# Weight rounding in a top-k attention and MLP kernel: the power of two by an exponential in bfloat16 on ScalarE

## The chip, the cores and the metric

The kernel runs on one core of a Trainium2 chip. The metric is the device time of one execution in microseconds, as the median of several runs. TensorE (PE) multiplies matrices, VectorE (DVE) and ScalarE (ACT) work element by element, GpSimd (POOL) does the same more slowly, and SyncE (SP) issues the DMA transfers.

## The reference, cut to what matters

```
scores = q @ k.T / sqrt(64)              # 8 batches x 8 heads, 576 x 576
keep the 32 largest of each row, softmax over them
attn_out = attn @ v                      # laid out as x: 4608 tokens x 512
h = x @ w_in                             # 512 x 2048
out = maximum(0.01 * h, h) @ w_out       # 2048 x 512
```

The inputs `w_in` and `w_out` arrive as 64-bit floats; the others are used as 32-bit floats. The kernel rounds the two weight matrices to 32 bits on the chip. This rounding is where the change lies.

## The kernel before, in words

**Three stages.** First the weights are loaded and rounded. Then 144 units of attention (128 query rows of two heads each) go through scores, top 32, softmax, transposition and the product with `v`. Whenever the tokens of a chunk (128 or 256) are complete, the MLP runs on them. The order of instructions on every engine is written out by hand: each engine works through its own queue in the order in which the program emits instructions, and waits on semaphores where data or buffers are missing. The MLP's matmuls are spread between those of attention by a budget, so that TensorE is fed throughout.

**Weight rounding.** `round_weights(n)` handles one of 16 pieces of 128 x 1024 values (pieces 0 to 7 are `w_in`, 8 to 15 `w_out`). Each 64-bit value arrives as four 16-bit words, 1 MB for a piece, in one of three `raw` buffers. The value is put together again as mantissa times a signed power of two:

- L119, GpSimd: the topmost word (sign, 11 bits of exponent, 4 bits of mantissa) is copied to `top`. It has two buffers, so the copy of piece n waits until piece n - 2 is done with it (L146).
- L120 and L122, ScalarE: the middle and the two low words become floats, in `dst` and `m_low`.
- L124, VectorE: shift and mask give the exponent, a number from 0 to 2047, as a 16-bit integer in `scale`.
- L126, VectorE: it is clamped to 896 to 1151, the range for which a power of two can be made by shifting bits.
- L128, ScalarE, pieces 0 to 13: (exponent - 896) x 128 is the bit pattern of that power of two in bfloat16. For pieces 14 and 15 VectorE does this (L130).
- L131 and L132, VectorE: the top mantissa bits as a bfloat16 between 1 and 2, and the sign bit alone.
- L142 to L144, TensorE: three matmuls with scaled identities add up the three parts of the mantissa in PSUM.
- L146 and L149, VectorE: sign and power of two are joined by an or, and the mantissa sum from PSUM is multiplied by the result.

**The order around it.** The loop at L484 interleaves three pieces. In step n the program emits piece n's part up to the first `yield` (L119 to L122), piece n - 1's part up to the second (L124 to L144), and piece n - 2's rest (L146, L149); then SP's queue gets the load of piece n + 3. So on VectorE one step is L124, L126, L131, L132 of one piece, then L146 and L149 of the piece before. On ScalarE it is L120 and L122 of one piece, then L128 of the piece before. The load of piece n + 3 takes the `raw` buffer of piece n, and waits until L119, L120 and L122 of piece n have read it.

In steps 6 to 9 the loads of four pairs of q and k (L162, L163, 0.59 MB a pair) stand in SP's queue behind the weights'. In step 13 `first_scores` of the first unit is emitted (TensorE L230, ScalarE copies L235), and in step 16 that of the second. The first `top_k` (VectorE, L244 to L252) stands behind the last L149 in VectorE's queue.

Of the kernel before, what the change touches and what calls it, by code (L numbers as in the profile page):

```python
# [1 line left out]

# [6 lines left out]
F32 = mybir.dt.float32  # L9
U32 = mybir.dt.uint32  # L10
U16 = mybir.dt.uint16
BF16 = mybir.dt.bfloat16
AF = mybir.ActivationFunctionType
ALU = mybir.AluOpType
# [5 lines left out]
def kernel(  # L20
# [13 lines left out]
    nc = tc.nc  # L34
    NPAIR, P, S = qT.shape
# [22 lines left out]
    const = ctx.enter_context(tc.tile_pool(name="const", bufs=1))  # L58
# [13 lines left out]
    ident_low = const.tile([P, P], BF16, name="ident_low")  # L72
    nc.vector.tensor_scalar(ident_low, ident, 2.0 ** -23, None, ALU.mult)

    w_in = [const.tile([P, DFF], F32, name=f"w_in{c}") for c in range(HP)]
    w_out = [const.tile([P, 4, DMODEL], F32, name=f"w_out{c}") for c in range(NFC // 4)]
    gT = const.tile([P, NFC, CHMAX], F32, name="gT")
# [3 lines left out]
    NPIECE = 2 * HP * DFF // WCH  # L81
# [3 lines left out]
    def piece(n):  # L85

        if n < NPIECE // 2:
            j, c = divmod(n, HP)
            return w_in[c][:, j * WCH:(j + 1) * WCH]
        f = 2 * (n - NPIECE // 2)  # L90
        return w_out[f // 4][:, f % 4:f % 4 + 2, :].rearrange("p g n -> p (g n)")
# [12 lines left out]
    def round_weights(n):  # L104

        raw = raw_of.pop(n)  # L110
        dst = piece(n)
        mid = raw[:, :, 2]
        low = raw.rearrange("p n w -> p (n w)").bitcast(U32).rearrange("p (n w) -> p n w", w=2)[:, :, 0]
        top = raws.tile([P, WCH], U16, name="top", bufs=2)
        scale = raws.tile([P, WCH], U16, name="scale", bufs=2)
        parts = work.tile([P, 2 * NKC - 1, P], F32, name="wT", bufs=3)
        parts = parts.rearrange("p c n -> p (c n)").bitcast(U16)
        m_top, m_low = parts[:, 0:WCH], parts[:, WCH:2 * WCH].bitcast(BF16)
        nc.gpsimd.tensor_copy(top, raw[:, :, 3])  # L119
        nc.scalar.activation(dst, mid, AF.Copy, bias=-7.0 - 2.0 ** -16, scale=2.0 ** -20)  # L120

        nc.scalar.activation(m_low, low, AF.Copy, bias=128.0, scale=2.0 ** -29)  # L122
        yield
        nc.vector.tensor_scalar(scale, top, 4, 0x7FF, ALU.logical_shift_right, ALU.bitwise_and)  # L124

        nc.vector.tensor_scalar(scale, scale, 1151.0, 896.0, ALU.min, ALU.max)  # L126
        if n < NPIECE - 2:
            nc.scalar.activation(scale, scale, AF.Copy, bias=-896.0 * 128, scale=128.0)  # L128
        else:
            nc.vector.tensor_scalar(scale, scale, 896.0, 128.0, ALU.subtract, ALU.mult)  # L130
        nc.vector.tensor_scalar(m_top, top, 0xF, 0x3F80, ALU.bitwise_and, ALU.bitwise_or)  # L131
        nc.vector.tensor_scalar(top, top, 0x8000, None, ALU.bitwise_and)  # L132
        if n < NPIECE - 4 or n % 2 == 0:
            tag, bufs = ("wide", 2) if n < NPIECE - 4 else ("narrow", 1)
            pw = ps_sc.tile([P, 2, 512], F32, name=tag, bufs=bufs)
            sums = [(pw[:, h, :], h * 512) for h in range(2)]
            ends = [(pw.rearrange("p h n -> p (h n)"), 0)]
        else:
            ends = sums = [(ps_ml.tile([P, 512], F32, name="pw", tag="ml"), h * 512) for h in range(2)]
        for pw, c in sums:  # L140
            at = slice(c, c + 512)
            nc.tensor.matmul(pw, ident_top, m_top[:, at].bitcast(BF16), start=True, stop=False)  # L142
            nc.tensor.matmul(pw, ident, dst[:, at], start=False, stop=False)
            nc.tensor.matmul(pw, ident_low, m_low[:, at], start=False, stop=True)  # L144
        yield
        nc.vector.tensor_tensor(scale, scale, top, ALU.bitwise_or)  # L146
        for pw, c in ends:
            at = slice(c, c + pw.shape[-1])
            nc.vector.tensor_tensor(dst[:, at], pw, scale[:, at].bitcast(BF16), ALU.mult)  # L149
# [319 lines left out]
    with tc.manual_schedule():  # L469
# [14 lines left out]
        for n in range(NPIECE + 2):  # L484
            for i in (n, n - 1, n - 2) if AS_WORDS else ():
                if 0 <= i < NPIECE:
                    if i == n:
                        rounding[i] = round_weights(i)
                    next(rounding[i], None)
            load_weights(n + 3)  # L490
            if 6 <= n < 6 + HP:
                load_qk(n - 6)
            elif n == NPIECE - 3:
                first_scores(steps[0])
            elif n == NPIECE:
                first_scores(steps[1])
            if n == NPIECE - 1:
                load_v(0)
                load_v(1)
# [132 lines left out]
```

## Time and profile before

| | before |
|---|---|
| median of 6 runs | 1476.02 us (1474.91 to 1477.42) |
| the profiled execution | 1476.83 us |
| its span in the trace | 1475.0 us |
| mean granted clock of TensorE | 0.981 |
| TensorE busy | 1392.9 us (94%) |
| VectorE busy | 1328.3 us (90%) |
| ScalarE busy | 1096.4 us (74%) |
| GpSimd busy | 1097.1 us (74%) |
| HBM read, written | 46.14 MB, 92.60 MB |
| L126, 16 instructions | 427 ns each, at 7.1 to 63.9 us |
| L128, 14 instructions | 1052 ns each |
| table loads on ScalarE | 1, 1283 ns, at 0.71 us |

How to read it: the span is what the hardware profiler recorded from the first instruction to the last, and the execution's own time is a little longer. Busy time is an average over three very different stages, so a stage has to be looked at by itself: a row of the timeline gives start, duration, engine, line, operation and, in brackets, how long the engine was idle before and what ended that.

### The profile page before, as it was taken

How to read it: one execution, taken by the hardware profiler on the slowest of the kernel's cores; microseconds unless marked ns; L12 is line 12 of the kernel's file. 1: busy time of each engine (PE TensorE's matmuls, PEld its weight loads, DVE VectorE, ACT ScalarE, POOL GpSimd, SP SyncE). 2: the span in 40 equal slices, each digit the busy share in tenths (PEclk: the TensorE clock that was granted, in tenths of full speed). 3: DMA queues.
4: the chain of work that ended last, by engine and by line, in shares of the span. 5: the costliest groups of instructions: out<-in, count | busy, mean ns of one | idle time of the engine just before them, and what ended most of it. 6: DMA issues, size and time to landing. Idle time of an engine off the chain costs nothing.

```text
span 1475.0 us, 24095 instructions
## 1 busy us (share of the span) xinstructions
PE 1392.9 (94%) x8059; PEld 926.5 (63%) x8059; DVE 1328.3 (90%) x3414; ACT 1096.4 (74%) x1979; POOL 1097.1 (74%) x742
## 2 busy tenths in 40 slices
PE   6715989999999999999999999999999999999998
PEld 2303547676766767676767666767676767676674
DVE  7999999999999999999999999999999999999600
ACT  8647887877788787877787877787877787877720
POOL 2278887887788888788878887888788888788700
PEclk9967999999999999999999999999999999999999
DMA  8724453655367464565566545575557556554510
GB/s 324 304 59 132 138 144 93 183 141 156 100 176 207 135 150 133 171 186 148 139 164 193 150 126 145 163 204 138 135 164 208 134 142 132 165 134 137 144 47 14
DMA packets 391420, 223.48 MB, mean 152 GB/s; under 512 B 336256, under 2 KB 336256, under 8 KB 389248
## 3 DMA queue, kind: packets, MB, share of 16 engines
q1 hardware_dynamic: 391296, 221.95, 53.8%
q8 instruction: 63, 1.03, 0.3%
q14 instruction: 61, 0.50, 0.1%
HBM read 46.14 MB, written 92.60 MB: 94 GB/s over the span
## 4 chain that ended last, share of the span: by engine, by line
PE 86%; DVE 12%; DMA 1%; issue 1%; ACT 0%; POOL 0%; DVEq 0%; ACTq 0%
PE pz L390 33%; PE ph L378 32%; PE wide L327 11%; PE wide L214 6%; DVE tops L249 4%; PE narrow L214 3%; DVE pairs L252 3%; DVE pairs L244 1%; DVE w_out L149 1%; DMA wT<-apart 1%; DVE w_in L149 1%; DVE scale L146 1%; DVE scale L124 0%; DVE scale L126 0%; DVE top L132 0%
## 5 line engine op out<-in xcount | busy, mean ns | idle before, releaser
L262 POOL TENSOR_SCALAR pen<-s_sb,tops 128x576 f32<-128x576 f32 x288 | 638.1, 2216 | 208.6 <-DVE tops L249 122.2
L249 DVE MAX8 tops<-pairs 128x8 f32<-128x288 f32 (+1 forms) x1152 | 635.9, 591 | 0.0
L390 PE MATMUL pz<-w_out,gT 128*128 128x512 f32 x1152 | 508.4, 596 | 0.0
L378 PE MATMUL ph<-x,w_in 128*128 128x256 f32 x2176 | 481.1, 381 | 0.0
L252 DVE MATCH_REPLACE8 pairs<-tops,pairs 128x288 f32<-128x288 f32 (+1 forms) x864 | 460.1, 538 | 0.0
L378 PEld LDWEIGHTS ph<-x,w_in 128*128 128x128 f32 x2176 | 410.7, 190 | 77.1 <-issue 22.9
L263 POOL TENSOR_TENSOR s_sb<-s_sb,pen 128x576 f32<-128x576 f32 x288 | 406.6, 1412 | 24.0
L390 PEld LDWEIGHTS pz<-w_out,gT 128*128 128x128 f32 x1152 | 215.3, 190 | 266.2 <-issue 264.3
L287 ACT COPY split<-s_sb 128x1152 uint16<-128x1152 uint16 x282 | 309.1, 1144 | 0.0
L278 ACT ACTIVATE s_sb<-s_sb,rz 128x576 f32<-128x576 f32 x288 | 207.0, 769 | 41.0 <-DVE rz L275 40.9
L266 ACT ACTIVATE s_sb<-s_sb,nbias 128x576 f32<-128x576 f32 x288 | 220.9, 767 | 12.5 <-POOL s_sb L263 12.5
L244 DVE TENSOR_TENSOR pairs<-s_sb 128x576 f32<-128x576 f32 x288 | 213.7, 780 | 9.9
L327 PEld LDWEIGHTS wide<-wT,vt 128*64 128x64 f32 x3200 | 160.8, 139 | 67.3 <-ACT s_sb L221 26.5
L327 PE MATMUL wide<-wT,vt 128*64 128x128 f32 (+1 forms) x3200 | 178.2, 268 | 24.6 <-ACT s_sb L221 21.8
L384 ACT ACTIVATE gT<-ph 128x512 f32<-128x512 f32 x136 | 80.6, 593 | 80.0 <-PE ph L378 80.0
L341 ACT COPY x<-wide 128x128 f32<-128x128 f32 (+1 forms) x160 | 32.1, 260 | 129.5 <-PE wide L327 129.4
L221 ACT COPY s_sb<-wide 128x704 f32<-128x704 f32 x142 | 107.1, 754 | 23.7 <-PE wide L214 23.6
L214 PE MATMUL wide<-kt,qt 64*128 64x352 f32 (+1 forms) x392 | 75.9, 503 | 27.2 <-ACT s_sb L221 23.6
L221 ACT COPY s_sb<-narrow 128x448 f32<-128x448 f32 x142 | 68.7, 536 | 1.3 <-PE narrow L214 0.7
L397 ACT COPY o_sb<-pz 128x512 f32<-128x512 f32 x36 | 21.1, 585 | 59.3 <-PE pz L390 59.3
L275 DVE RECIPROCAL rz<-ze 128x2 f32<-128x2 f32 x144 | 22.4, 155 | 45.4 <-ACT ze L271 45.2
L252 DVE MATCH_VALUE_LOAD pairs<-tops,pairs 128x8 f32 x864 | 62.6, 72 | 0.0
(62 smaller groups left out, 623.8 us busy)
## 6 DMA issues: line engine op xcount, KB each, us to landing
apart<-split SPq DMA_DIRECT2D x282, 288.0 KB, 2.1
raw<-in_weights_dram SPq DMA_DIRECT2D x16, 1024.0 KB, 6.2
vt<-in_vk_dram SPq DMA_DIRECT2D x32, 320.0 KB, 3.3
out_dram<-o_sb SPq DMA_DIRECT2D x36, 256.0 KB, 2.0
qt<-in_qT_dram SPq DMA_DIRECT2D x20, 288.0 KB, 3.3
kt<-in_kT_dram SPq DMA_DIRECT2D x20, 288.0 KB, 3.6
raw<-in_qT_dram SPq DMA_DIRECT2D x12, 288.0 KB, 3.2
raw<-in_kT_dram SPq DMA_DIRECT2D x12, 288.0 KB, 3.5
```

What stands on the lines that cost most here:

```text
L214: nc.tensor.matmul(to[r0:r0 + u.rows, i, :], qt[d, u.q0:u.q0 + u.rows], kt[d, k0:k1], start=True, stop=True)
L244: nc.vector.tensor_tensor(pairs[:, :, n, :], u.both[:, :, 0:HS], u.both[:, :, HS:S], op)
L249: nc.vector.max(out=u.tops[:, i, r, :], in_=rest[i])
L252: nc.vector.match_replace(out=rest[i], in_to_replace=u.tops[:, i, r, :], in_values=rest[i], imm_value=LOWEST)
L262: nc.gpsimd.tensor_scalar(pen, u.s[i], u.tops[:, i, ROUNDS - 1, 7:8], MASKED, ALU.is_lt, ALU.mult)
L263: nc.gpsimd.tensor_tensor(u.s[i], u.s[i], pen, ALU.add)
L266: nc.scalar.activation(u.s[i], u.s[i], AF.Exp, bias=u.nbias[:, i:i + 1], scale=SCALE, accum_out=u.z[:, i:i + 1])
L278: nc.scalar.activation(u.s[i], u.s[i], AF.Copy, bias=0.0, scale=u.rz[:, i:i + 1])
L287: nc.scalar.copy(split, pairs[:, :, h])
L327: nc.tensor.matmul(po[side * D:(side + 1) * D, o, :], vt[:, c, side, :], u.wT[:, c + side * NKC if c + 1 < NKC else c, r:r + n], start=(c ...
L378: nc.tensor.matmul(ph[:, i, 0:n], w_in[c][:, f * P:(f + 1) * P], x[c][:, 0:n], start=(c == 0), stop=(c == HP - 1),)
L390: nc.tensor.matmul(pz[0:m, 0:DMODEL], gT[:, f, r0:r0 + m], w_out[f // 4][:, f % 4, :], start=(f == 0), stop=(f == NFC - 1),)
```

## The change

ScalarE now computes 2 to the power (exponent - 1023) as an exponential, exp(ln 2 x exponent - 1023 ln 2), and writes it into the same 16-bit words as a bfloat16 number; before, it computed the bit pattern as an integer. The bias is read from a new 128 x 1 tile, `least`, that GpSimd fills once at the start. The clamp on VectorE remains only for pieces 14 and 15, whose power of two VectorE makes by bits as before.

```
+    LN2 = math.log(2.0)
+    least = const.tile([P, 1], F32, name="least")
+    nc.gpsimd.memset(least, -1023.0 * LN2)
...
         nc.vector.tensor_scalar(scale, top, 4, 0x7FF, ALU.logical_shift_right, ALU.bitwise_and)
-
-        nc.vector.tensor_scalar(scale, scale, 1151.0, 896.0, ALU.min, ALU.max)
         if n < NPIECE - 2:
-            nc.scalar.activation(scale, scale, AF.Copy, bias=-896.0 * 128, scale=128.0)
+
+            nc.scalar.activation(scale.bitcast(BF16), scale, AF.Exp, bias=least, scale=LN2)
         else:
+
+            nc.vector.tensor_scalar(scale, scale, 1151.0, 896.0, ALU.min, ALU.max)
             nc.vector.tensor_scalar(scale, scale, 896.0, 128.0, ALU.subtract, ALU.mult)
```

More of the change, by code (lines that the diff above doesn't have):

```diff
@@ L1 @@
+import math
 from contextlib import ExitStack
```

## The prediction

> **What bounds the kernel now.** I read the page's busy slices first, then the windows view by stage, the wait view of TensorE, the timeline of the weight stage engine by engine, the weight stage's waits, and last the groups of ScalarE.
>
> First the page's busy tenths in 40 slices of 36.9 us, then two rows of the windows view (busy us and counts of PE, PEld, DVE, ACT, POOL, then granted clock, DMA share, GB/s).
>
> ```profile
> PE   6715989999999999999999999999999999999998
> ...
> DVE  7999999999999999999999999999999999999600
> ```
>
> ```profile
> 70.00:140.00 70.00, 21.71 (x152) 15.45 (x151) 69.48 (x182) 40.78 (x76) 52.98 (x37) 0.66 0.31 85
> ...
> 200.00:1365.00 1165.00, 1159.30 (x7031) 792.89 (x7031) 1119.51 (x2916) 917.10 (x1696) 948.45 (x635) 1.00 0.57 153
> ```
>
> Three stages follow one another. The weights are rounded until 69.4 us. Then VectorE picks the first top 32 without a gap (69.48 of 70 us) while TensorE waits for it (21.71 of 70 us busy). From about 140 us TensorE is the full engine: 1159.30 of 1165 us, and the chain that ended last is its matmuls. Nothing between 70 us and the end is tied to an absolute time: the first `top_k` starts behind the last L149 on VectorE, and TensorE's long stretch starts behind the first `top_k`s. A weight stage that ends x us earlier should end the program x us earlier, so the question is what paces this stage.
>
> The timeline of one step of it (start us, duration, engine, line, idle before), for VectorE, ScalarE and GpSimd:
>
> ```profile
> 33.14 0.43 DVE L124 TENSOR_SCALAR scale<-top 128x1024 uint16<-128x1024 uint16 x1
> 33.60 0.43 DVE L126 TENSOR_SCALAR scale<-scale 128x1024 uint16<-128x1024 uint16 x1
> 33.94 0.42 DVE L131 TENSOR_SCALAR wT<-top 128x1024 uint16<-128x1024 uint16 x1
> 34.40 0.43 DVE L132 TENSOR_SCALAR top<-top 128x1024 uint16<-128x1024 uint16 x1
> 34.74 0.69 DVE L146 TENSOR_TENSOR scale<-scale,top 128x1024 uint16<-128x1024 uint16 x1
> 35.53 1.23 DVE L149 TENSOR_TENSOR w_in<-wide,scale 128x1024 f32<-128x1024 f32 x1
> 36.87 0.43 DVE L124 TENSOR_SCALAR scale<-top 128x1024 uint16<-128x1024 uint16 x1
> ```
>
> ```profile
> 34.06 1.06 ACT L128 ACTIVATE scale<-scale 128x1024 uint16<-128x1024 uint16 x1 [0.57 <-DVE scale L126]
> 35.03 1.14 ACT L120 ACTIVATE w_out<-raw 128x1024 f32<-128x1024 uint16 x1
> 36.08 1.12 ACT L122 ACTIVATE wT<-raw 128x1024 bf16<-128x1024 uint32 x1
> ```
>
> ```profile
> 35.49 1.14 POOL L119 COPY top<-raw 128x1024 uint16<-128x1024 uint16 x1 [2.58 <-DVE scale L146]
> ```
>
> VectorE has no gap: its step is 36.87 - 33.14 = 3.73 us, and L126 holds 33.60 - 33.14 = 0.46 of it (0.43 of work and the wait for its own predecessor's result). ScalarE is idle 0.57 us in it, waiting for L126.
>
> Waits of the weight stage, ScalarE's timeline at its end, and a row of the windows view there:
>
> ```profile
> ACT w_out L120 <- DMA raw<-in_weights_dram: 2.7, 3, 1.2
> ...
> DVE scale L146 <- ACT scale L128: 0.2, 1, 0.2
> ```
>
> ```profile
> 51.51 1.14 ACT L120 ACTIVATE w_out<-raw 128x1024 f32<-128x1024 uint16 x1 [1.17 <-DMA raw<-in_weights_dram]
> ...
> 53.60 1.04 ACT L128 ACTIVATE scale<-scale 128x1024 uint16<-128x1024 uint16 x1
> 56.97 1.18 ACT L235 COPY s_sb<-wide 128x576 f32<-128x576 f32 x2 [2.32 <-PE wide L230]
> ...
> 60.11 1.07 ACT L128 ACTIVATE scale<-scale 128x1024 uint16<-128x1024 uint16 x1
> ```
>
> ```profile
> 40.00:45.00 5.00, 3.66 (x11) 1.17 (x9) 4.58 (x9) 3.74 (x4) 1.51 (x2) 1.00 1.04 416
> ```
>
> The reader is to see two near limits. Pieces 11 to 13 come late to ScalarE (three waits, 2.7 us), because four q/k pairs are loaded between them and the 16 DMA engines are full (share 1.04 at 416 GB/s). And the last ACT L128, of piece 13, ends at 60.11 + 1.07 = 61.18 us, just before the L146 that needs it (VectorE's timeline: 61.26).
>
> **The change, part by part.** The profiled execution took 1476.83 us (span 1475.0, 1.83 around it), 0.81 over the median of 1476.02; gains are worked out in its trace and taken from the median.
>
> *VectorE loses 14 x L126.* L131 does not read `scale`, so it will follow L124 as it now follows L126, after 0.34 us; each piece's step falls by 0.46 to 3.27 us. The ceiling is 14 x 0.46 = 6.4 us. Piece 0's share counts, through TensorE: its matmuls start behind L131 and end when L149 may begin (13.22 us). Piece 1's does not: VectorE then waits for ScalarE (the 0.2 us row) and for those matmuls. From piece 2 each counts, so L124 of piece n comes 0.46 x (n - 1) earlier: piece 12 by 5.06, at 46.69; piece 13 by 5.52, at 49.95.
>
> *ScalarE's copy becomes an exponential with a bias read from a tile* (groups of instructions: count, busy us, mean ns, idle before).
>
> ```profile
> L266 ACT ACTIVATE s_sb<-s_sb,nbias 128x576 f32<-128x576 f32 x288 | 220.9, 767 | 12.5 <-POOL s_sb L263 12.5
> ...
> L306 ACT COPY wT<-wide 128x1024 f32<-128x1024 f32 x3 | 3.0, 1012 | 2.6 <-PE wide L300 2.6
> ...
> L306 ACT COPY wT<-wide 128x128 f32<-128x128 f32 x3 | 0.8, 277 | 0.0
> ```
>
> No exponential of 1024 elements from 16-bit words is in the trace. The nearest row is L266, an exponential with a bias tile, 767 ns for 576; the two L306 rows give (1012 - 277) / 896 = 0.82 ns an element, so 767 + 448 x 0.82 = 1134 ns against L128's 1052: +0.08. Bounds: 1012 ns (L306, -0.04) and 1182 ns (the longest L120, +0.13). When ScalarE doesn't wait, its step is 3.02 us (L128 at 16.17 to L128 at 19.19); it becomes 3.10, still under 3.27. The 0.08 is covered by what is left of ScalarE's idle time, 0.17 a step; without that cover it is 14 x 0.08 = 1.1 us.
>
> *A memset of 128x1 on GpSimd.* L619's memsets take 0.10 us, and GpSimd sits idle from 1.3 to 5.5 us for the first transfer; without that cover, 0.1 us. The exponential also waits for it, 8 us after it is done. The exponential's other wait moves from L126 to L124, so it is shorter; behind it in ScalarE's queue stand the next piece's L120 and L122, and L146 waits for it.
>
> *What comes earlier with it.* TensorE's share of a step is 2.75 us (34.42 to 37.18), under 3.27. GpSimd's copy waits for L146, and L124 for the copy: 1.14 + 0.69 + the VectorE work between is 3.55 of 3.73 now and shrinks by the same 0.46. SP issues the load of piece n + 3 when copy n has ended, with the q/k loads queued behind it. Piece 9's load is issued with copy 6, at 29.2 us, now 5 x 0.46 = 2.3 us earlier (pieces 0 and 2 to 5). From it on the DMA engines are full: the landings of pieces 11, 12 and 13 (43.24, 47.22, 51.51 us, where ScalarE resumed) are 4.1 us apart for a piece and a pair, 1.64 MB, which is 400 GB/s. So these landings come only 2.3 us earlier: piece 12 at 44.92, piece 13 at 49.21, while VectorE would want them 5 us earlier. The slack that hid this shrinks away:
> - Piece 12: L120, L122 and the exponential of piece 11 end 2.09 + 1.13 us after landing (2.09 is 51.51 to 53.60), at 48.14. VectorE would reach L146 at 46.69 + 1.14 = 47.83. Stall 0.35.
> - Piece 13: exponential of piece 12 ends at 49.21 + 3.22 = 52.43. VectorE reaches L146 at 51.55 (L124 at 50.41, behind GpSimd's copy). Stall 0.92; L146 at 52.47 instead of 57.07, gain 4.6.
> - The clamp of piece 13 is gone from VectorE, where L124 of piece 14 follows at 54.60 and L146 could start at 56.67. ScalarE's queue (exponential 12, two copies L235, L120, L122, exponential 13) ends at 51.30 + 1.05 + 1.06 + 1.06 + 1.02 + 1.13 = 56.62. They tie: no further stall.
>
> The weight stage ends 4.6 us earlier, and the median becomes 1476.02 - 4.6 = 1471.4.
>
> One rule of the Trainium skill speaks against that rate. The page "DMA: Bandwidth & Descriptors", section "Where 436 GB/s comes from", puts loads from HBM at about 358 GB/s for a core; here the 40 to 45 us row has 416, so the measurement decides. By the page's figure piece and pair would take an estimated 4.6 us instead of 4.1, pieces 11 to 13 would land 1 to 2 us later and the gain would be near 3.
>
> **The rivals.**
> - *The transfers keep up.* If the loads, asked for earlier, land as much earlier (the share of 0.76 to 0.94 before 35 us is some room), only ScalarE's queue at piece 13 is left: VectorE's gain at L149 of piece 11 is 12 x 0.46 = 5.5, less 0.08: 5.4 us, and up to 6.4 if that queue has slack. 1470.6, at best 1469.6. Against: the share stands at 0.96 to 1.04 from 35 us.
> - *The transfers decide all.* If ScalarE's chain behind piece 13's landing has no slack beyond the 2.3 us that L146 had (landing + 5.56 now, 3.26 needed), or the DMA engines lose rate, the gain is only the landings' own shift, 2.3: 1473.7.
> - *It doesn't arrive at the end.* TensorE has 98% of its work from 140 us on; if its written-out order gives the gain back in new waits (it has 7 us of waits from 200 us on), the time stays at 1476.
> - *Slower: the exponential and the copies evict each other's tables.* Place: ScalarE, between L122 and L128. A table load took 1.28 us at the start; two for each of 14 pieces make ScalarE's step 3.10 + 2.56 = 5.66 us, against VectorE's present 3.73: some 13 x 1.9 = 25 us, 1501. It decides from 0.63 us of extra ScalarE work a piece (3.73 - 3.10). Against: the page has one table load in a program with 288 exponentials between copies and Prelus. The Trainium skill, "ScalarE: Activation LUTs", section "What ACT_TABLE_LOAD costs", prices every switch at 2.66 us, by which two a piece would be an estimated 5.3 us a piece.
>
> **How the numbers follow.** My forecast (gain 3.5 to 5.1) 0.58; transfers keep up 0.18; transfers decide 0.13; nothing arrives 0.06; slower 0.05. About 0.2% (3 us) is what a measurement of this kernel can tell from no change. Faster by more: 0.58 + 0.18 = 0.76. Within: 0.13 + 0.06 = 0.19. Slower: 0.05. The range goes from the ceiling (1469.6) less 0.2 for the runs' spread to the transfers' case (1473.7) and 0.3 more: 1469.4 to 1474.0, which leaves out the last two cases and edges.
>
> **What would show it.** Right: no L126 but two; L124 to L124 3.27 us apart between pieces 3 and 10; the exponential at 1.1 to 1.2 us; one table load; VectorE's L146 waiting for ScalarE once or twice, about 1.3 us in all, near 48 and 52 us; `top_k`'s first L244 at 64.8 instead of 69.42. Wrong: a step that stays above 3.4 us, further table loads, waits of several us for `raw`, or a first L244 that is early with an end that isn't.

## The result and the profile after

| | before | after |
|---|---|---|
| median | 1475.69 us (36 runs) | 1473.04 us (18 runs, 1470.64 to 1473.93) |
| ratio to before | | 0.9978, 95% interval 0.9972 to 0.9984 |
| the profiled execution, its span | 1476.83, 1475.0 us | 1473.77, 1471.8 us |
| first `top_k` instruction on VectorE | 69.42 us | 66.01 us |
| from there to the end of the span | 1405.6 us | 1405.8 us |

The change makes the kernel 0.22% faster, about 3.2 us (2.4 to 4.1 by the interval); the two medians alone are 2.65 us apart. The forecast was a gain of 4.6 us. All of the gain is made before the first `top_k`, where 3.4 of the forecast 4.6 us arrived; the rest of the program lasts as long as before. The diff adds lines: the exponent's shift is now L129, the exponential L132, the mantissa bits L137, the sign L138, the or L152, the product L155, the first `top_k` line L250, and on ScalarE L120 and L122 are L125 and L127.

The busy tenths on the page after:

```profile
PE   7716989999999999999999999999999999999998
...
DVE  6899999999999999999999999999999999999600
```

And the windows view (busy us and counts of PE, PEld, DVE, ACT, POOL; clock, DMA share, GB/s):

```profile
70.00:140.00 70.00, 21.88 (x133) 14.70 (x130) 69.38 (x180) 41.13 (x76) 55.99 (x38) 0.66 0.34 93
200.00:1365.00 1165.00, 1162.37 (x7043) 795.12 (x7042) 1119.11 (x2918) 916.00 (x1694) 949.11 (x635) 1.00 0.57 153
```

The three stages are the same: VectorE without a gap behind the weights, then TensorE full.

VectorE's timeline of one late step of the weight stage, after (start us, duration, engine, line, idle before):

```profile
43.99 0.43 DVE L129 TENSOR_SCALAR scale<-top 128x1024 uint16<-128x1024 uint16 x1
44.33 0.42 DVE L137 TENSOR_SCALAR wT<-top 128x1024 uint16<-128x1024 uint16 x1
44.79 0.43 DVE L138 TENSOR_SCALAR top<-top 128x1024 uint16<-128x1024 uint16 x1
45.77 0.69 DVE L152 TENSOR_TENSOR scale<-scale,top 128x1024 uint16<-128x1024 uint16 x1 [0.55 <-ACT scale L132]
46.56 1.23 DVE L155 TENSOR_TENSOR w_out<-wide,scale 128x1024 f32<-128x1024 f32 x1
47.89 0.43 DVE L129 TENSOR_SCALAR scale<-top 128x1024 uint16<-128x1024 uint16 x1
```

The clamp is gone, and L137 follows L129 after 0.34 us. But this step is 3.90 us long: the or L152 waits for ScalarE's exponential. The waits of the stage, after:

```profile
ACT w_out L125 <- DMA raw<-in_weights_dram: 3.4, 5, 0.8
...
DVE scale L152 <- ACT scale L132: 2.6, 4, 0.8
...
DVE scale L129 <- DVE w_in L155: 0.5, 1, 0.5
```

ScalarE's timeline shows what the exponential waited for: it stands behind L125 and L127 of the next piece, and these wait for its transfer (pieces 10 to 13).

```profile
38.52 1.15 ACT L125 ACTIVATE w_out<-raw 128x1024 f32<-128x1024 uint16 x1 [0.78 <-DMA raw<-in_weights_dram]
...
42.51 1.17 ACT L125 ACTIVATE w_out<-raw 128x1024 f32<-128x1024 uint16 x1 [0.74 <-DMA raw<-in_weights_dram]
...
46.50 1.15 ACT L125 ACTIVATE w_out<-raw 128x1024 f32<-128x1024 uint16 x1 [0.76 <-DMA raw<-in_weights_dram]
...
50.40 1.15 ACT L125 ACTIVATE w_out<-raw 128x1024 f32<-128x1024 uint16 x1 [0.70 <-DMA raw<-in_weights_dram]
```

They are 4.0 us apart, and VectorE's steps behind them 3.9 to 4.0. The loads themselves take longer from issue to landing (least, median and longest of the 16 weight pieces, before and then after):

```profile
DMA to landing us min/median/max: 4.7/6.2/8.9
```

```profile
DMA to landing us min/median/max: 4.9/7.1/9.6
```

### The profile page after: what moved, and what is told of

It reads as the page before. It is cut to its first block, busy times and chain, and to the rows that moved or that the text cites. A ratio compares the mean times of both kernels' runs of the same rounds, so it can differ in the third digit from the quotient of the medians.

```text
span 1471.8 us, 24082 instructions
## 1 busy us (share of the span) xinstructions
PE 1394.1 (95%) x8059; PEld 927.6 (63%) x8059; DVE 1322.4 (90%) x3400; ACT 1097.3 (75%) x1979; POOL 1097.1 (75%) x743
## 4 chain that ended last, share of the span: by engine, by line
PE 84%; DVE 11%; DMA 3%; ACT 1%; issue 1%; SPq 0%; POOL 0%; DVEq 0%; ACTq 0%
PE pz L396 32%; PE ph L384 31%; PE wide L333 10%; PE wide L220 6%; DVE tops L255 4%; PE narrow L220 3%; DVE pairs L258 3%; DMA wT<-apart 1%; DVE pairs L250 1%; DMA raw<-in_weights_dram 1%; ACT split L293 1%; DMA apart<-split 1%; DVE w_in L155 1%; DVE w_out L155 0%; DVE scale L152 0%
## 5 line engine op out<-in xcount | busy, mean ns | idle before, releaser
L250 DVE TENSOR_TENSOR pairs<-s_sb 128x576 f32<-128x576 f32 x288 | 213.4, 779 | 10.0
L347 ACT COPY x<-wide 128x128 f32<-128x128 f32 (+1 forms) x160 | 32.1, 260 | 129.9 <-PE wide L333 129.9
L258 DVE MATCH_VALUE_LOAD pairs<-tops,pairs 128x8 f32 x864 | 62.5, 72 | 0.0
```

What stands on the lines that cost most here:

```text
L250: nc.vector.tensor_tensor(pairs[:, :, n, :], u.both[:, :, 0:HS], u.both[:, :, HS:S], op)
L258: nc.vector.match_replace(out=rest[i], in_to_replace=u.tops[:, i, r, :], in_values=rest[i], imm_value=LOWEST)
```

## The experiments

The theory: VectorE's step did fall by 0.46 us, and the landings of the weight pieces, held up by the four q/k pairs among them, took part of it back (transfers theory). The main rival: the dearer exponential holds up VectorE's or (ScalarE theory). Beside the medians, the table gives the start of the first `top_k` in the profiled execution, which shows the stage alone and is not blurred by the 1405 us behind it. It is the start in one execution, and that need not be a typical one: E3's and E6's profiled executions were the slowest of their runs, E7's and E9's the fastest, 1.2 to 2.7 us from the median. Each ratio is to the kernel before in the same session, whose median was 1475.41 us for E1 to E4, 1475.01 for E5 to E8 and 1474.86 for E9 and E10, so medians of different sessions are not to be compared as they stand.

| kernel | median us | ratio to before, interval | first `top_k` us | from there to the span's end |
|---|---|---|---|---|
| E1 no clamp, integer copy | 1471.96 | 0.9979, 0.9969 to 0.9988 | 65.96 | 1404.1 |
| E2 clamp, exponential | 1475.43 | 1.0001, 0.9992 to 1.0011 | 69.58 | 1404.8 |
| E3 change, late pairs | 1470.77 | 0.9968, 0.9956 to 0.9979 | 65.18 | 1404.9 |
| E4 before, late pairs | 1475.15 | 0.9997, 0.9988 to 1.0006 | 69.64 | 1405.2 |
| E5 change, no sign | 1472.78 | 0.9983, 0.9974 to 0.9992 | 67.11 | 1404.2 |
| E6 no sign, late pairs | 1470.34 | 0.9965, 0.9953 to 0.9977 | 64.19 | 1405.7 |
| E7 change, late pairs, new order | 1468.63 | 0.9956, 0.9944 to 0.9969 | 61.46 | 1404.1 |
| E8 as E7, no clamp at all | 1468.08 | 0.9954, 0.9940 to 0.9967 | 61.85 | 1404.4 |
| E9 change, new order | 1471.34 | 0.9977, 0.9968 to 0.9986 | 63.16 | 1403.7 |
| E10 before, late pairs, new order | 1470.85 | 0.9973, 0.9964 to 0.9982 | 64.66 | 1404.8 |

**E1 and E2: the two halves of the change alone.**

```
E1, on the change:
-            nc.scalar.activation(scale.bitcast(BF16), scale, AF.Exp, bias=least, scale=LN2)
+            nc.scalar.activation(scale, scale, AF.Copy, bias=-896.0 * 128, scale=128.0)
E2, on the change:
+        nc.vector.tensor_scalar(scale, scale, 1151.0, 896.0, ALU.min, ALU.max)
         if n < NPIECE - 2:
...
-            nc.vector.tensor_scalar(scale, scale, 1151.0, 896.0, ALU.min, ALU.max)
```

> The clamp of the first 14 pieces is gone, and ScalarE keeps its integer copy instead of the exponential. Transfers theory (the landings of pieces 9 to 13 cap the gain): the same time as the change, about 1473 (-2.7 to -3.2 against before), since the exponential's 0.08 us sits beside waits for landings; at most 0.3 us better, from three copies that stand behind a landing. ScalarE theory (the exponential's price holds VectorE's L152 up): the full 5.4 us, 1470.3.

> The exponential alone: VectorE keeps all 16 clamps. Transfers theory: VectorE's step stays 3.73 us and ScalarE's 3.10 is hidden in it, so 0 to +0.2 us against before, about 1475.8. ScalarE theory: slower by 14 x 0.08 = 1.1 us or more.

E1's ratio and its first `top_k` are those of the change (0.9979 and 0.9978; 65.96 and 66.01), and E2 is the kernel before (1.0001). Leaving out the clamp is worth everything; making the power of two by an exponential changes the time by nothing that these runs can tell. The ScalarE theory falls. The exponential's group in the profile after:

```profile
L132 ACT ACTIVATE scale<-scale,least 128x1024 bf16<-128x1024 uint16 x14 | 16.0, 1140 | 0.0
...
L125 ACT ACT_TABLE_LOAD x1 | 1.3, 1283 | 0.7 <-PEq L625 0.7
```

It takes 1140 ns, and there is still one table load.

**E3 and E4: three pairs loaded behind the last weight piece.**

```
-            if 6 <= n < 6 + HP:
-                load_qk(n - 6)
-            elif n == NPIECE - 3:
+            if n == 6:
+                load_qk(0)
+            elif NPIECE - 4 <= n < NPIECE - 1:
+                load_qk(n - (NPIECE - 5))
+            if n == NPIECE - 3:
                 first_scores(steps[0])
```

> The change, with the q/k pairs 1 to 3 (1.77 MB) loaded behind the last weight piece instead of between pieces 10 and 13. Transfers theory: the waits for landings of pieces 10 to 13 go, VectorE's step stays 3.26 us to piece 12, the first top_k instruction starts at 64.0 +- 0.4 instead of 66.01, and the time is 1475.7 - 5.4 = 1470.3. If the landings were late for another reason than these pairs (late already at pieces 6 to 9), about half of that: first top_k at 65, 1472. ScalarE theory: no change from 1473.

> The kernel before, with the same three pairs loaded behind the last weight piece. Transfers theory: ScalarE's waits for landings (2.7 us) go, but VectorE paced the stage, so the time stays within 0.4 us of 1475.7. If the transfers had cost the kernel before something too, it is 1 to 2 us faster.

E4 is the kernel before (0.9997): with the clamp, VectorE hid the transfers. E3 gains 4.7 us instead of 3.2, though the intervals of the two ratios overlap. But for 0.42 us at piece 9 its steps stay at 3.26 us to piece 14, whose L129 comes at 53.60 us instead of 55.78 in the change, and ScalarE's waits for pieces from 8 on fall from 3.4 to 1.2 us. So the late landings cost the change about 2.2 us at that point. Not all of this is the pairs' doing: up to piece 9 the two kernels load the same, and yet piece 9 took 5.2 us from issue to landing in E3's execution and 7.4 in the change's (more of this below). But the first `top_k` came at 65.18, not at 64.0. Part of it was lost at the end, where TensorE's timeline in E3 shows the last piece:

```profile
60.10 0.49 PE L148 MATMUL pw<-wT,ident_top 128*128 128x512 bf16 x1 [2.00 <-DVE wT L137]
60.38 1.92 PE L149 MATMUL pw<-w_out,ident 128*128 128x512 f32 x2
62.09 0.63 PE L150 MATMUL pw<-wT,ident_low 128*128 128x512 bf16 x1
```

The windows view of E3 at the same place:

```profile
58.00:60.00 2.00, 0.10 (x1) 0.00 (x0) 1.83 (x5) 0.21 (x1) 0.04 (x1) 1.00 1.03 399
60.00:62.00 2.00, 1.90 (x3) 0.69 (x3) 1.86 (x4) 0.00 (x0) 0.00 (x0) 0.56 1.05 403
62.00:64.00 2.00, 2.00 (x5) 0.92 (x4) 1.73 (x3) 0.00 (x0) 0.00 (x0) 0.59 1.04 393
```

TensorE idled 2.00 us for the last piece's mantissa bits, its granted clock fell to 0.56 to 0.59 (means of 2 us), and two matmuls of L149 took 1.92 us where they take 1.02 otherwise. VectorE waited 0.74 us for them, 0.42 us for the exponential of piece 13, and 0.42 us once more at L129 of piece 9 (told of below). Without these three, 65.18 would be 63.6.

**E5 and E6: one more instruction less on VectorE, with the pairs among the weights and behind them.**

```
-        nc.vector.tensor_scalar(top, top, 0x8000, None, ALU.bitwise_and)
+        if n >= NPIECE - 2:
+            nc.vector.tensor_scalar(top, top, 0x8000, None, ALU.bitwise_and)
...
-        nc.vector.tensor_tensor(scale, scale, top, ALU.bitwise_or)
+        nc.vector.tensor_tensor(scale, scale, top, ALU.bitwise_or if n >= NPIECE - 2 else ALU.bitwise_and)
```

> The change, and for pieces 0 to 13 also without the instruction that isolates the sign bit (the or behind it becomes an and, so the weights' scales are not the reference's). VectorE's step would fall by another 0.46 us, to 2.80. Transfers theory: the landings of pieces 9 to 13 pace the stage already, so the first top_k instruction stays at 65.0 to 66.0 us (66.01 in the change) and the time at 1472.0 to 1473.0. If VectorE still paced most of the stage: first top_k near 61, 1468.

> The same with q/k pairs 1 to 3 behind the last weight piece. VectorE's step 2.80, so ScalarE's 3.12 or the transfers of one piece in 3.2 us pace it. Transfers theory: first top_k 1.0 to 2.5 us earlier than the 65.18 of the run with late pairs and the sign kept. ScalarE theory says the same with 3.12 a piece: 16 pieces end at about 63.5. If neither bounds it: 60.

For pieces 0 to 13 these two kernels leave out the isolation of the sign, so their weights are not the reference's; only their time is of use. E5 has 14 x 0.46 us less to do on VectorE than the change, and its first `top_k` starts no earlier: 67.11 us, later than the forecast 65 to 66 even; the time is that of the change. What VectorE no longer does it waits, as its row in the waits of E5 shows:

```profile
DVE scale L153 <- ACT scale L132: 9.0, 13, 1.3
```

Thus VectorE did not pace the stage any more. In E6 the first `top_k` came at 64.19, 1.0 earlier than E3's, at the lower end of what was expected; VectorE there waits 0.23 us for ScalarE in most steps, whose own step is 3.12 us. So three limits lie close together: VectorE's 3.26, ScalarE's 3.12, and the transfers.

**E7 and E8: VectorE makes the mantissa bits first.** E7 is E3 with one line moved; E8 also drops the last two clamps.

```
E7, on E3:
+        nc.vector.tensor_scalar(m_top, top, 0xF, 0x3F80, ALU.bitwise_and, ALU.bitwise_or)
         nc.vector.tensor_scalar(scale, top, 4, 0x7FF, ALU.logical_shift_right, ALU.bitwise_and)
...
-        nc.vector.tensor_scalar(m_top, top, 0xF, 0x3F80, ALU.bitwise_and, ALU.bitwise_or)
E8, on E7:
-            nc.vector.tensor_scalar(scale, scale, 1151.0, 896.0, ALU.min, ALU.max)
```

> Late pairs, and VectorE makes the mantissa bits (the operand of the first matmul) ahead of the exponent. In the run with late pairs TensorE idled 2.00 us before the last piece, its clock then stood at 0.56 to 0.59 for 3.4 us, and VectorE waited 0.74 us for it. Clock theory: the idle time falls to about 1.1 us, the clock stays at 1.00, the wait goes: first top_k at 64.4 instead of 65.18, time 0.7 us less (1470.0). If the idle time was not the reason: 65.2 again.

> As the run before it, and the last two clamps are gone as well. Piece 14's 0.46 us is lost, because the or behind it waits for ScalarE's exponential of piece 13; piece 15's counts: first top_k 0.5 us earlier than in the run before it, at 63.9; time 1469.5. If ScalarE did not hold it: 0.9 us earlier.

E7's first `top_k` came at 61.46, 3 us before what was expected. Part of that is the execution: E7's profiled one was its fastest and E3's its slowest. By the ratios, 0.9968 and 0.9956, the moved line is worth some 1.8 us, with intervals that overlap. TensorE's clock stayed at 1.00 and the 0.74 us went, as forecast; the rest I had not seen. VectorE's timeline in E3, and then in E7:

```profile
22.53 1.23 DVE L155 TENSOR_TENSOR w_in<-wide,scale 128x1024 f32<-128x1024 f32 x1
23.86 0.43 DVE L129 TENSOR_SCALAR scale<-top 128x1024 uint16<-128x1024 uint16 x1
...
25.79 1.23 DVE L155 TENSOR_TENSOR w_in<-wide,scale 128x1024 f32<-128x1024 f32 x1
```

```profile
21.62 1.23 DVE L155 TENSOR_TENSOR w_in<-wide,scale 128x1024 f32<-128x1024 f32 x1
22.76 0.42 DVE L129 TENSOR_SCALAR wT<-top 128x1024 uint16<-128x1024 uint16 x1
...
24.68 1.23 DVE L155 TENSOR_TENSOR w_in<-wide,scale 128x1024 f32<-128x1024 f32 x1
```

Behind the product L155 the exponent's instruction starts after 1.33 us, the mantissa's after 1.14. The exponent is written into the `scale` buffer that this very product reads (the tile has two buffers), so it has to wait until the product is done; the mantissa bits go elsewhere. The step falls from 3.26 to 3.06 us, then ScalarE's 3.12 paces. The extra 0.42 us is missing in E7 too. E8's time differs from E7's by nothing that can be measured, against the 0.5 us expected, and its first `top_k` is 0.39 us later: in its execution the landings of pieces 9 and 10, which its edit doesn't touch, held it up (0.29 and 0.77 us of waits at the or).

**E9 and E10: the order without the late pairs, and without the change.** E9 is the change with E7's moved line, E10 is E4 with it.

> The change, with only VectorE's order altered (mantissa bits ahead of the exponent), the q/k pairs where they were. VectorE's step is 3.06 us in that order. Transfers theory: the landings pace pieces 9 to 13, so first top_k within 0.7 us of the change's 66.01 and the time within 0.7 us of 1473. If the order is worth what it was with late pairs (61.46 instead of 65.18): 62.5 and 1469.5.

> The clamp and the integer copy as before, with late pairs and VectorE's new order, so that only the change of this case separates it from the run that has all three (first top_k 61.46, 0.9956 of before). VectorE's step 3.72 - 0.2 = 3.52 against the 3.12 that ScalarE allows there: 14 pieces x 0.40 = 5.2 to 5.6 us. Expected: first top_k 66.7 to 67.1, time 1473.0. If the transfers still capped: 64 or less.

E9's ratio is the change's, 0.9977, as the transfers theory says: the order alone wins nothing that the times can tell. But its profiled execution, the fastest of its 11 (1468.66 to 1473.65), has the first `top_k` at 63.16, 2.2 us before the lower end expected and near the rival's 62.5: in it ScalarE waited for two landings from piece 8 on instead of five, as the waits of E9 show.

```profile
ACT w_out L125 <- DMA raw<-in_weights_dram: 2.2, 2, 1.2
```

The landings seem to differ from one execution to the next. E9's times spread over 5.0 us, those of E10, in which VectorE paces most of the steps, over 2.0.

E10 missed, by 2 us: 64.66 and 1470.85. With the clamp in place the new order saves 0.32 us a step, not 0.2 (its step is 3.40 instead of 3.72), because the sign's instruction, which overwrites `top`, now stands behind the clamp, which doesn't touch `top`, and follows after 0.34 us; behind the mantissa's, which reads `top`, it came after 0.46. So order and late pairs without the change are worth 0.9973, about as much as the change. What the change adds to them, E7 against E10, is 3.2 us at the first `top_k`: the 3.40 us of VectorE against the 3.12 that ScalarE allows, 0.28 x 12 = 3.4. By the ratios, 0.9956 and 0.9973, it is 2.5 us.

## Why the prediction was right or wrong

The time (1473.04) lies in the range (1469.4 to 1474.0), and the sign was right. The gain was sized too high, 4.6 us for about 3.2, and that is less than the 3.5 to 5.1 us of the forecast's own case: it lies between this case and the rival "the transfers decide all" (2.3 us). Step by step:

- **An earlier end of the weight stage ends the program earlier by as much: right.** From the first `top_k` to the end of the span it is 1403.7 to 1405.8 us in all twelve kernels, while the first `top_k` itself moves by 8 us. (TensorE has 95% of its work from 140 us on, 1322.32 of 1392.9 us, not the 98% that the prediction gives; nothing else is worked out from it.)
- **VectorE's step falls by 0.46 to 3.27 us: right.** It is 3.26 from piece 3 to piece 8. Up to there L129 comes 3.06 us earlier (33.81 instead of 36.87).
- **The exponential costs 0.08 us and is hidden: right.** 1140 ns against the 1134 worked out, and E2 shows no loss. The slower rival had no place: one table load.
- **Piece 0's share counts: partly.** L129 of piece 2 came 0.29 instead of 0.46 us earlier, since the first piece landed 0.16 us later in that execution.
- **The landings of pieces 11 to 13 come 2.3 us earlier: this step failed.** They came 0.73, 0.72 and 1.11 us earlier (42.51, 46.50, 50.40). I took the shift of piece 9's issue, which was nearly right (27.1 instead of 29.2), and assumed that its landing shifts with it. It landed at 27.1 + 7.4 = 34.5 us, later than the 29.2 + 4.7 = 33.9 of before.
- **Two stalls of 0.35 and 0.92 us: undersized with it.** There were three at the or, of 0.64, 0.70 and 0.66 us beyond the usual distance of 0.34 from L138 (at 45.77, 49.73, 53.66), and 0.42 us at L129 of piece 9, 2.4 us instead of 1.3. With 0.29 and 12 x 0.46 before them this gives 0.29 + 5.5 - 2.4 = 3.4, the gain at the first `top_k`.

What went before piece 9 is seen in the windows view. After:

```profile
16.00:28.00 12.00, 10.60 (x32) 3.94 (x30) 11.06 (x19) 11.72 (x13) 4.53 (x4) 1.00 0.92 339
28.00:34.00 6.00, 5.39 (x16) 2.14 (x16) 5.51 (x10) 6.00 (x6) 2.26 (x2) 1.00 0.97 335
34.00:50.00 16.00, 12.43 (x38) 4.95 (x38) 13.41 (x24) 12.99 (x13) 4.57 (x4) 1.00 1.02 414
```

And before:

```profile
16.00:28.00 12.00, 9.11 (x27) 3.53 (x27) 11.15 (x20) 10.83 (x12) 3.41 (x3) 1.00 0.80 290
28.00:34.00 6.00, 4.49 (x14) 1.64 (x12) 5.49 (x10) 4.92 (x5) 2.29 (x2) 1.00 0.85 325
34.00:50.00 16.00, 11.71 (x35) 4.71 (x36) 14.85 (x28) 13.24 (x13) 4.56 (x4) 1.00 1.01 400
```

A piece every 3.26 us asks for 1.05 MB / 3.26 us = 322 GB/s, and with weights alone the DMA engines moved 335 to 339 at shares of 0.92 to 0.97. I had read the shares below 1 before 35 us as some room. But each piece was issued while the one before was still in flight, and pieces 6 to 8 took 7.3, 7.0 and 6.2 us instead of 4.9, 4.8 and 4.7. So loads stood in the queue before the pairs came, instead of gathering with them. E3 bears this out in part: without the pairs the landings of pieces 11 to 13 took 6.2 to 7.0 us from the issue, not 8.9 to 9.6.

The traces of the other kernels, one execution of each, show where this backlog stands (us from issue to landing):

| kernels | VectorE's usual step | pieces 3 to 5 | pieces 6 to 9 |
|---|---|---|---|
| before, E2, E4 | 3.72 | 6.3 to 7.0 | 4.6 to 4.9 |
| E10 | 3.40 | 6.7 to 7.2 | 6.8 to 7.5 |
| change, E1 | 3.26 | 6.6 to 7.3 | 6.2 to 7.7 |
| E3 | 3.26 | 5.8 to 6.4 | 5.2 to 6.5 |
| E5 to E8 | 2.8 to 3.12 | 5.8 to 7.2 | 5.1 to 7.7 |
| E9 | 3.12 | 5.5 to 5.9 | 4.7 to 5.0 |

The loads of the first pieces leave a backlog in every trace. At 3.72 us a step it is gone by piece 6. At 3.40 and less piece 6 still takes 6.5 to 7.4 us, but for E9, whose execution began with the least. The windows from 10 to 16 us show the difference at the start, in the change and then in E9:

```profile
10.00:16.00 6.00, 6.00 (x15) 2.73 (x14) 4.10 (x8) 5.55 (x7) 1.10 (x1) 1.00 1.02 332
```

```profile
10.00:16.00 6.00, 6.00 (x19) 2.67 (x19) 4.91 (x8) 6.00 (x7) 1.99 (x2) 1.00 0.97 400
```

E9 asks for its pieces sooner than the change and has the pairs in the same place, and its pieces 11 to 13 landed 3.6 to 4.4 us before those of the kernel before. In E3 piece 9 landed at 32.1 us, 1.8 before. So the shift that I forecast does come where there is no backlog, or little, and the change's profiled execution had one. Why the engines, about equally full, moved so much less in one execution than in the other is not shown, and no run here changes the backlog alone.

The prediction's rule from the Trainium skill ("DMA: Bandwidth & Descriptors", "Where 436 GB/s comes from", about 358 GB/s from HBM) would have given a gain near 3, closer than mine. Yet it is not the cause here: where the landings paced, from 34 to 50 us, 414 GB/s were moved. Why weights alone went at only 335 to 339 at shares of 0.92 to 0.97 is open.

Also open is the 0.42 us at L129 of piece 9: it stands at the same instruction in the change, E1 and E3, and is missing in the kernel before, E2, E4 and E5 to E9; E10 has one like it at a product. No run here shows what it waits for.

## What to carry to other kernels

A gain on the pacing engine is bounded by the next limit, and that limit can move when work is asked for sooner. Rate and share of the DMA engines did not tell how near it was: from 16 to 28 us the change had 339 GB/s at 0.92 with landings of 6.2 to 7.3 us, and E9 332 at 0.91 with 4.7 to 5.0. The time from issue to landing did tell. Two instructions of VectorE cost a pause where the second writes what the first used or reads what it wrote (0.46 us from start to start instead of 0.34 for these short ones), so an order in which an independent one stands there can be worth about as much as an instruction removed (E10's ratio of 0.9973 against E4's 0.9997). A start time in the profile behind the changed stage shows tenths of a microsecond where whole times differ by 0.2%, but it is that of one execution, here up to 2.7 us from the median.

## What the runs showed of the hardware that I had not expected

TensorE's clock fell to half in two executions. TensorE had been idle for 2.00 us in E3 (58.10 to 60.10) and for 2.26 us in E6 (56.96 to 59.22); in both the granted clock went from 1.00 to 0.50 at 60.2 us and back at 63.6, 3.4 us later. In E6 it fell 1.0 us after the matmuls had begun again. But 2.31 us of idle time in E5 left it at 1.00, as 1.80 us did in the change. The rows of E5 behind that gap, with two matmuls of L150 (L149 in E3) in 1.02 us and not 1.92:

```profile
49.60 0.38 PE L149 MATMUL narrow<-wT,ident_top 128*128 128x512 bf16 x1 [2.31 <-DVE wT L137]
49.82 1.02 PE L150 MATMUL narrow<-w_out,ident 128*128 128x512 f32 x2
```

So the length of the idle time alone doesn't decide whether the clock falls; what else does is not tested here. The Trainium skill, "TensorE: Matmul & The Clock Gate", section "Part 1: The HAM clock gate (the "warmup" mystery)", names windows of about 3.4 us, both for falling and for rising again; the 3.4 us at half clock agree with it, and the falls came after idle times shorter than that.
